# Sliding-window attention and SiLU feed-forward on one core: a replanned order, tile 0's activations in another buffer, fewer idle products

## The chip, the core and the metric

The kernel runs on one core of a Trainium2 chip. The core has a matrix engine (TensorE, PE in the profile, whose weight loads are listed apart as PEld), a vector engine (VectorE, DVE), an activation engine (ScalarE, ACT), a general engine (GpSimd, POOL) and a queue engine (SyncE, SP). Each runs its own list of instructions in order and waits on semaphores for the others. Transfers are issued by POOL, SP or ACT and moved by 16 DMA engines. PE writes its products to PSUM, eight banks of 128 x 512 fp32 values. The metric is device time in microseconds, the median of several runs.

## The reference

Two stages follow each other: causal attention with a window of 64 keys, for 8 batches of 8 heads, 576 positions and 64 values a head; then a feed-forward layer over all 4608 tokens.

```python
scores = scale * np.matmul(q, k.transpose(0, 1, 3, 2))
mask = (rel >= 0) & (rel < window)          # rel = query position - key position, window = 64
scores = np.where(mask, scores, -1000000000.0)
attn = np.exp(scores - max); attn = attn / (attn.sum(-1) + 1e-09)
x = (attn @ v).transpose(0, 2, 1, 3).reshape(4608, 512)
h = x @ w_in                                 # 512 x 2048
out = (h / (1 + np.exp(-h))) @ w_out         # 2048 x 512
```

## The kernel before

**Tiles.** The 4608 tokens are nine tiles of 512. A block is 64 query positions; a tile has 8 blocks. A quad is four of the eight heads. A visit is the attention of one quad for 4 or 8 blocks: `scores` on PE (a block against the 128 keys before its end), `exp` on ACT, a mask on DVE, `values` on PE, then on DVE the reciprocal of the sums, the product with it, and a transpose (`turn_out`, called "cross" in the plan) into the tile's input `xts`. In tile 0 the mask is a product of `block` with `ident` that is added to the scores on PE.

**Products.** Tile 0 uses plain products: `first_plain` makes 16 groups of 128 x 512 (a pair of columns of `w_in` for one half of the tokens, 8 products of 256 columns each, over four chunks of the contraction; chunks 0 and 1 come from quad 0, chunks 2 and 3 from quad 1), `silu_plain` makes the activations on ACT, and `second_plain` makes 64 products of 512 columns into four banks. Tiles 1 to 8 use a scheme with seven products instead of eight, with sums of weights (`wsum1`, `wsum2`), of tokens (`xsum`) and of activations (`gsum`) made on DVE, and a copy between banks on ACT ("fork"), a kept copy ("keep") and additions on DVE ("join") between the products. The stretch in which tile 0 is finished while the attention for tile 1 is made is called the bridge here.

**Order.** Every operation is recorded in a plan; `ORDER` is a written list of about 1590 words, each an operation's number, its engine and its banks. The instructions of an engine stand in the order of that list, so an engine's first waiting instruction holds all behind it. The loads of queries, keys, values and weights are all issued by POOL.

**Idle products.** PE begins with products of zeros (`warm`, 128 x 512), and more of them stand between the first scores; there are 36.

**Names.** `nat_87` and `nat_86` are the keys and the queries of batch 0 for quad 0, `nat_89` and `nat_88` those for quad 1; 90 to 93 are those of batch 1. `vv_98` are the values of batch 0. `w_in_sb_63` to `66` are four column parts of `w_in`, each loaded in two transfers (one for chunks 0 and 1, one for 2 and 3). `es_84` and `es_85` are the exponentials of quads 0 and 1. ACT holds one table of functions at a time; exp and SiLU need different ones, and a table load stands ahead of the first activation that needs another.

## Time and profile before

| | before |
|---|---|
| time, median of 3 runs | 277.2 us (276.77 to 277.22) |
| span of the profiled execution | 275.0 us |
| PE busy | 264.7 us (96%) |
| DVE busy | 214.0 us (78%) |
| ACT busy | 195.6 us (71%) |
| POOL busy | 129.7 us (47%) |
| table loads on ACT | 18, 1283 ns each |
| first product of tile 0, first product of tile 1 | 17.74 us, 52.23 us |

The profile is of one execution; what it gives as time is the span from the first to the last instruction, 2.2 us under the median of the runs. A row of the timeline has its start in us, its length, engine, line, operation, the tiles written and read, the count of merged instructions, and in brackets how long the engine sat idle before it and what ended that. A busy PE is not PE at its peak: a product counts as busy until its result is out, so products that follow each other with small waits still look busy.

### The profile page before, as it was taken

Reading aid. Unit: us, or ns where it says so; the run is one execution under the profiler, and the core shown is the slowest. Engines: PE = TensorE matmul, PEld = TensorE weight load, DVE = VectorE, ACT = ScalarE, POOL = GpSimd, SP = SyncE. Lnnn points to the kernel's source line nnn. Section 1 sums busy time; section 2 is a strip of 40 time slices with the busy share of each in tenths; the row PEclk is TensorE's granted clock in tenths of the full one; section 3 lists DMA queues with packets and bytes.
Section 4 is the critical chain, followed back from the end, with each engine's and each line's share of the span. In section 5 each row is a group of like instructions: output and inputs, shape, how many; then the busy total and the mean of one; then the engine's idle time right before and its main releaser. Section 6 shows DMA issues by size and latency. Waiting matters only on the chain.

```text
span 275.0 us, 10018 instructions
## 1 busy us (share of the span) xinstructions
PE 264.7 (96%) x4335; PEld 218.0 (79%) x4342; DVE 214.0 (78%) x426; ACT 195.6 (71%) x361; POOL 129.7 (47%) x194
## 2 busy tenths in 40 slices
PE   7978999999999999999999999999999999999993
PEld 2557844688888888888888888888888888888882
DVE  3757578999996898889799999988867967824741
ACT  1555993699749993987499958893888489537910
POOL 7944566988959758596387335940000000000000
PEclk9999999999999999999999999999999999999999
DMA  6999999999999959999979998990400040003004
GB/s 106 167 190 210 198 191 172 144 198 157 118 151 209 127 56 97 242 122 87 93 179 159 83 126 122 136 121 2 155 0 2 6 155 0 2 29 127 0 2 157
DMA packets 101631, 31.62 MB, mean 115 GB/s; under 512 B 92368, under 2 KB 95440, under 8 KB 101584
## 3 DMA queue, kind: packets, MB, share of 16 engines
q0 software_dynamic: 96128, 21.51, 86.1%
q1 hardware_dynamic: 5456, 9.44, 9.7%
q8 instruction: 35, 0.57, 0.9%
q14 instruction: 12, 0.10, 0.1%
HBM read 42.99 MB, written 9.44 MB: 191 GB/s over the span
## 4 chain that ended last, share of the span: by engine, by line
PE 88%; ACT 4%; DVE 4%; issue 1%; ACTq 0%
PE room L519 36%; PE room L507 35%; PE room L292 4%; PE room L323 4%; PE room L450 4%; PE room L895 4%; PE room L464 2%; ACT es L307 2%; DVE o L338 1%; ACT L307 1%; ACT g L461 1%; DVE es L314 1%; DVE xt L442 1%; PE room L285 1%; ACT L461 0%
## 5 line engine op out<-in xcount | busy, mean ns | idle before, releaser
L529 ACT ACTIVATE g<-room 128x512 bf16<-128x512 f32 x96 | 53.6, 605 | 4.5 <-PE room L507 4.1
L507 PEld LDWEIGHTS <-wsum 128*128 128x128 bf16 x512 | 49.9, 98 | 7.2 <-issue 1.0
L519 PEld LDWEIGHTS <-gsum 128*128 128x128 bf16 x512 | 49.1, 98 | 6.2 <-DVE gsum L496 0.2
L507 PE MATMUL room<-xsum,wsum 128*128 128x256 bf16 x384 | 53.3, 272 | 0.5 <-ACT es L307 0.3
L307 ACT ACTIVATE es<-room 128x512 bf16<-128x512 f32 (+1 forms) x88 | 39.1, 533 | 14.2 <-PE room L292 9.6
L519 PE MATMUL room<-wsum,gsum 128*128 128x256 bf16 x384 | 48.4, 273 | 0.0
L507 PEld LDWEIGHTS <-w_in_sb 128*128 128x128 bf16 x384 | 37.2, 98 | 4.7
L519 PEld LDWEIGHTS <-g 128*128 128x128 bf16 x384 | 36.7, 98 | 4.6
L526 DVE TENSOR_TENSOR room<-room,part 128x512 f32<-128x512 f32 (+1 forms) x41 | 27.8, 684 | 13.7 <-ACT part L523 3.5
L227 POOL DMA_DIRECT2D nat<-in_k_dram x48 | 30.0, 631 | 15.1 <-DVE kT L265 11.4
L507 PE MATMUL room<-xt,w_in_sb 128*128 128x256 bf16 x256 | 36.8, 273 | 0.0
L519 PE MATMUL room<-w_out_sb,g 128*128 128x256 bf16 x256 | 35.7, 273 | 0.0
L227 POOL DMA_DIRECT2D nat<-in_q_dram x48 | 29.9, 637 | 9.7 <-DVE qT L268 6.1
L523 ACT COPY ot<-room 128x512 f32<-128x512 f32 (+1 forms) x23 | 13.3, 582 | 28.6 <-PE room L519 21.5
L235 POOL DMA_DIRECT2D vv<-in_v_dram x32 | 29.6, 940 | 5.0 <-DMA nat<-in_k_dram 1.7
L523 ACT COPY room<-room 128x512 f32<-128x512 f32 x40 | 23.3, 592 | 12.1 <-PE room L507 10.8
L526 DVE TENSOR_TENSOR fin<-room,part 128x512 f32<-128x512 f32 x32 | 21.6, 683 | 9.0 <-PE room L507 6.1
L523 ACT COPY part<-room 128x512 f32<-128x512 f32 x40 | 23.6, 598 | 6.4 <-PE room L519 3.2
L241 POOL DMA_DIRECT2D vv<-in_v_dram x24 | 22.3, 934 | 12.0 <-PE room L323 11.5
L314 DVE TENSOR_TENSOR es<-es,strip 128x1024 bf16<-128x1024 bf16 (+1 forms) x36 | 21.9, 626 | 6.7 <-ACT es L307 6.4
L338 DVE TENSOR_TENSOR o<-room,recips 128x896 bf16<-128x896 f32 (+2 forms) x36 | 25.9, 726 | 0.8
L496 DVE TENSOR_TENSOR gsum<-g,gsum 128x512 bf16<-128x512 bf16 x64 | 25.1, 415 | 0.4
(75 smaller groups left out, 376.8 us busy)
## 6 DMA issues: line engine op xcount, KB each, us to landing
out_dram<-ot SPq DMA_DIRECT2D x16, 512.0 KB, 3.9
vv<-in_v_dram POOLq DMA_DIRECT2D x56, 128.0 KB, 5.0
nat<-in_k_dram POOLq DMA_DIRECT2D x48, 72.0 KB, 4.0
nat<-in_q_dram POOLq DMA_DIRECT2D x48, 72.0 KB, 3.7
w_in_sb<-in_moe_w_in_dram POOLq DMA_DIRECT2D x8, 256.0 KB, 9.2
w_out_sb<-in_moe_w_out_dram POOLq DMA_DIRECT2D x8, 256.0 KB, 9.0
nat<-in_k_dram POOLq DMA_DIRECT2D x4, 288.0 KB, 8.0
nat<-in_q_dram POOLq DMA_DIRECT2D x4, 288.0 KB, 8.2
```

What stands on the lines that cost most here:

```text
L227: queue[e].dma_start(out=nats[b % 2][a][kk][32 * h:32 * h + 32].rearrange("p (n x) -> p n x", n=NB), in_=(q, k)[kk][b, 4 * a + h].rearrang ...
L235: queue[e].dma_start(out=vv[b % 2][:, :, 2 * g + 1, 0:D], in_=v[b, :, 128 * g:128 * g + 128].rearrange("h p d -> p h d"))
L241: queue[e].dma_start(out=vv[b % 2][:, :, 2 * g, 0:D], in_=v[b, :, 128 * g - 64:128 * g + 64].rearrange("h p d -> p h d"))
L307: nc.scalar.activation(out=es_part(a, blocks)[:, h], in_=banks[bank.idx][:, 0:64 * n], func=ACTF.Exp, scale=scale)
L314: nc.vector.tensor_mul(t, t, strip[:, s:s + n].rearrange("k n i -> k (n i)").unsqueeze(1).to_broadcast([128, 2, 64 * n]))
L338: nc.vector.tensor_mul(out, at_values(bank, n)[:, :, :, 0:D], recips[:, w:w + 2 * n].rearrange("k (t n) -> k t n", t=bank.wide).unsqueeze( ...
L496: nc.vector.tensor_sub(out=dst[2 * i - 1], in0=g(1, 2 - i), in1=dst[i - 1])
L507: nc.tensor.matmul(banks[bank.idx][:, 256 * i:256 * i + 256], lhsT=lhs(z, i), rhs=rhs(z), start=(start and i == 0 and z == 0), stop=(z == ...
L519: nc.tensor.matmul(banks[bank.idx][:, 256 * m:256 * m + 256], lhsT=lhs(m, i), rhs=rhs(i), start=(start and i == 0 and m == 0), stop=(stop ...
L523: copies[e](out=dst, in_=src)
L526: nc.vector.tensor_add(out=dst, in0=bank, in1=part)
L529: nc.scalar.activation(out=g_tile(pair, 256 * t, 256 * t + 256), in_=src.rearrange("k (f t) -> k f t", f=2), func=ACTF.Silu)
```

## The change

- `run` takes a function `load`, which it calls ahead of the first ACT operation of another table: an activation of one column of `tiny`. The table load then stands ahead of that activation and no longer ahead of the operation itself.
- The first constants are filled on DVE (`const_fills`) and no longer on POOL; `ident` is made with one select instead of two.
- Tile 0's input lies in `xts[0]` by halves of the tokens (`by_half`), its activations lie in the space of `gsum` (`g_first`) and no longer in `gall`.
- All 16 groups of `first_plain` are split in two parts, one for quad 0's chunks and one for quad 1's, and a part waits only for the token half that it reads. Before, four groups of the first half were split.
- Copies of `vv` may go to ACT or DVE alike; the last tile's stores may be issued by ACT.
- The `ORDER` list is another one throughout, with 16 idle products, all at the start.

```diff
+            if engine == "A" and op["table"] not in (None, table):
+                table = op["table"]
+                load(table)
...
 ORDER = (
-    "1D 9G 2D 74P7 3D 11G 69P2 72P5 13G 67P0 15G 68P1 73P6 5G 70P3 71P4 19G 7D 78P3 81P6 82P7 86P3 6G 10D 77P2 89P6 90P7 75P0 17G 76P1 80P5 12D 83P0 79P4 "
...
+    "0D 9G 69P2 95P7 11G 92P4 72P7 86P7 1D 2D 18G 91P4 17G 67P4 4D 5G 7D 94P4 3D 15G 6G 13G 10D 97P7 83P2 68P0 75P1 73P0 99P2 70P3 78P0 12D 20G 19G 29G "
...
-        nc.gpsimd.memset(strip[:, 0], 1.0)
...
     def const_ident(_):
-        nc.gpsimd.memset(ident, 1.0)
-        nc.gpsimd.affine_select(out=ident, in_=ident, compare_op=ALU.is_ge, fill=0.0, base=0, channel_multiplier=1, pattern=[[-1, 128]])
-        nc.gpsimd.affine_select(out=ident, in_=ident, compare_op=ALU.is_ge, fill=0.0, base=0, channel_multiplier=-1, pattern=[[1, 128]])
+        nc.gpsimd.affine_select(out=ident, in_=ident, compare_op=ALU.not_equal, fill=1.0, base=0, channel_multiplier=1, pattern=[[-1, 128]])
+
+    def const_fills(_):
+        nc.vector.memset(strip[:, 0], 1.0)
+        nc.vector.memset(ident, 0.0)
+        nc.vector.memset(tiny, 0.0)
...
+    def by_half(t):
+        return t.rearrange("k c t -> k (c t)").rearrange("k (h c t) -> k h c t", h=2, c=4)
...
-                    rhs=xts[j % NXT][:, c, lo:hi], start=(i == 0 and c == 0), stop=(c == 3), skip_group_check=True)
+                    rhs=by_half(xts[0])[:, lo // 256, c], start=(i == 0 and c == 0), stop=(c == 3), skip_group_check=True)
+
+    g_first = gsum.rearrange("k u n f t -> k (u n f t)").rearrange("k (g f t) -> k g f t", g=8, f=2)
...
-            nc.scalar.activation(out=g_tile(pr, lo, hi), in_=src[:, i], func=ACTF.Silu)
+            nc.scalar.activation(out=g_first[:, pr, :, lo:hi], in_=src[:, i], func=ACTF.Silu)
...
-                if j == 0 and k_ == 0 and g0 < SPLIT:
-                    half = [x for nb in range(4) for x in xt_done[nb][:1]] + [win[ft // 2][0] for ft in fts]
...
+                half = [x for nb in range(lo // 64, hi // 64) for x in xt_done[nb][:1]] + [win[ft // 2][0] for ft in fts]
...
-            st = p.add({"SP": 0.45}, lambda e, i=i, r0=r0, r1=r1, lo=lo, hi=hi: store(e, j, 2 * i + r0, 2 * i + r1, lo, hi), deps, 0,
+            st = p.add({"SP": 0.45, "ACT": 0.4} if last else {"SP": 0.45}, lambda e, i=i, r0=r0, r1=r1, lo=lo, hi=hi: store(e, j, 2 * i + r0, 2 * i + r1, lo, hi), deps, 0,
...
-    p.run(ORDER)
+    p.run(ORDER, lambda table: nc.scalar.activation(out=tiny[:, 1:2], in_=tiny[:, 0:1], func={"exp": ACTF.Exp, "silu": ACTF.Silu}[table]))
```

The list's rows tell a reader nothing, so three places are shown as the engines' instructions stand, without their waits.

POOL's list at the start of the program, before: all keys and queries of batch 0, then the masks, then the values.

```order
L224 DMA nat_87<-in_k_dram 128x1152
L224 DMA nat_86<-in_q_dram 128x1152
L224 DMA nat_89<-in_k_dram 128x1152
L224 DMA nat_88<-in_q_dram 128x1152
L184 MEMSET strip 128x64
L185 ISA
L185 AFFINE_SELECT strip<-strip 128x64
L187 AFFINE_SELECT strip<-strip 128x64
L235 DMA vv_98<-in_v_dram 128x8x64
L191 MEMSET ident 128x128
```

The same place after the change:

```order
L230 DMA nat_87<-in_k_dram 128x1152
L230 DMA nat_86<-in_q_dram 128x1152
L241 DMA vv_98<-in_v_dram 128x8x64 x2
L188 ISA
L188 AFFINE_SELECT strip<-strip 128x64
L190 AFFINE_SELECT strip<-strip 128x64
L230 DMA nat_88<-in_q_dram 128x1152
L194 AFFINE_SELECT ident<-ident 128x128
L230 DMA nat_89<-in_k_dram 128x1152
L241 DMA vv_98<-in_v_dram 128x8x64 x2
L251 DMA w_in_sb_63<-in_moe_w_in_dram 128x2x512
```

Two transfers of values moved ahead of quad 1's queries and keys, and the masks behind those two.

DVE's list from the first transposes to the first result of the attention, before:

```order
L255 STREAM_TRANSPOSE kT_97<-nat_89 128x18x32
L258 STREAM_TRANSPOSE qT_95<-nat_88 128x9x64
L273 COPY vv_98<-vv_98 64x8x64
L205 MEMSET vv_99 128x72
L206 MEMSET vv_99 64x8x32
L275 COPY vv_98<-vv_98 64x8x64
L273 COPY vv_98<-vv_98 64x8x64
L275 COPY vv_98<-vv_98 64x8x64
L334 RECIPROCAL recips<-room 128x8
```

The same place after the change:

```order
L261 STREAM_TRANSPOSE kT_96<-nat_87 128x18x32
L264 STREAM_TRANSPOSE qT_94<-nat_86 128x9x64
L279 COPY vv_98<-vv_98 64x8x64 x2
L281 COPY vv_98<-vv_98 64x8x64 x2
L264 STREAM_TRANSPOSE qT_95<-nat_88 128x9x64
L261 STREAM_TRANSPOSE kT_97<-nat_89 128x18x32
L281 COPY vv_98<-vv_98 64x8x64
L340 RECIPROCAL recips<-room 128x8
```

The four copies of the first values now stand ahead of quad 1's transposes, and these stand between the first values and their reciprocal.

ACT's list at the end of tile 8, before:

```order
L529 ACTIVATE g<-fin_81 128x2x256
L523 COPY room<-room 128x512
L529 ACTIVATE g<-room 128x2x256 x2
L523 COPY part_80<-room 128x512
L523 COPY ot<-room 128x2x256
L523 COPY ot<-room 128x256
```

The same place after the change:

```order
L534 COPY part_80<-room 128x512
L544 DMA out_dram<-ot 128x2x256
L534 COPY ot<-room 128x256
L534 COPY ot<-room 128x2x256
L544 DMA out_dram<-ot 128x2x256
L534 COPY ot<-room 128x2x256
L534 COPY ot<-room 128x256
```

Two stores moved from SP's list into ACT's, and two output copies from DVE's into ACT's.

On PE, the list after the change has 16 idle products, then the scores of quad 0 for all eight blocks, its first values, quad 1's first scores, two parts of `first_plain`, the values of quad 0's second half, quad 1's other scores and values with three more parts among them, and then 25 parts in a row, the first of which also needs quad 1's half. Before, quad 0's scores, quad 1's scores and three of the four values stand with 11 idle products among them, ahead of the first part. In the bridge the list has four times 7 of the 64 second products and a scores step, then 8, two parts of `first_plain`, 2, two values, 8, two values and 17.

48 lines of the change are left out of this document (21 added, 27 removed), and 118 rows, old and new, of the table ORDER.

## Prediction

> **What bounds the kernel now.** I read the page's head, its slices and the chain first, then busy time by stage.
>
> ```profile
> span 275.0 us, 10018 instructions
> PE 264.7 (96%) x4335; PEld 218.0 (79%) x4342; DVE 214.0 (78%) x426; ACT 195.6 (71%) x361; POOL 129.7 (47%) x194
> DMA  6999999999999959999979998990400040003004
> PE 88%; ACT 4%; DVE 4%; issue 1%; ACTq 0%
> ```
>
> ```profile
> 0.00:17.70 17.70, 14.68 (x274) 7.27 (x275) 9.19 (x21) 8.93 (x21) 13.43 (x28) 1.00 1.19 146
> 34.20:52.20 18.00, 17.01 (x284) 8.12 (x288) 14.99 (x38) 11.56 (x26) 12.57 (x21) 1.00 1.43 163
> 195.00:222.00 27.00, 27.00 (x479) 23.64 (x477) 21.31 (x42) 20.65 (x38) 0.00 (x0) 1.00 0.16 60
> ```
>
> From left: stretch, length, busy time of PE, PEld, DVE, ACT, POOL with counts, granted clock, DMA, GB/s. In the middle PE is busy for the whole stretch and carries the chain: there only fewer products or smaller waits could help, and the change removes no real product. What can be won lies ahead of tile 0's products, in the bridge, and behind the last product. In the first two the DMA digit is 9, so transfers pace the start.
>
> ```profile
> 1.39 7.60 PE L895 MATMUL room<-fill 128*128 128x512 bf16 x24 [1.39 <-DVE fill L213]
> 5.58 1.25 DVE L255 STREAM_TRANSPOSE kT<-nat 128x576 f32<-128x576 f32 x1 [0.48 <-DMA nat<-in_k_dram]
> 7.06 1.21 DVE L258 STREAM_TRANSPOSE qT<-nat 128x576 f32<-128x576 f32 x1 [0.22 <-DMA nat<-in_q_dram]
> 9.36 0.42 PE L292 MATMUL room<-qT,kT 32*128 32x64 bf16 x32
> 11.86 0.29 DVE L273 COPY vv<-vv 64x512 bf16<-64x512 bf16 x1 [0.74 <-DMA vv<-in_v_dram]
> 15.50 0.70 POOL L245 DMA_DIRECT2D w_in_sb<-in_moe_w_in_dram  x1 [1.21 <-DMA w_in_sb<-in_moe_w_in_dram]
> 20.24 0.54 POOL L248 DMA_DIRECT2D w_out_sb<-in_moe_w_out_dram  x1 [0.77 <-DMA w_in_sb<-in_moe_w_in_dram]
> 17.21 0.60 PE L323 MATMUL room<-vv,es 128*32 128x65 bf16 x52 [1.58 <-issue]
> 22.42 7.91 PE room L450 x71
> 30.61 3.67 PE L450 MATMUL room<-xt,w_in_sb 128*128 128x256 bf16 x32
> 52.23 1.04 PE L507 MATMUL room<-xt,w_in_sb 128*128 128x256 bf16 x8
> ```
>
> Transfers land one after the other: quad 0's keys and queries by 5.58 and 7.06, then quad 1's two and the first two transfers of values, these by 11.86, later the `w_in` parts. POOL's issue at 15.50 was released by the first of these parts, that at 20.24, three issues on, by the fourth. The first scores stand behind the idle products, which run to 1.39 + 7.60 = 8.99. PE becomes dense at 22.42 (that row is the chain's). Of tile 0's 128 first products 71 + 32 = 103 follow there, so 25 were done.
>
> **The start.** The bytes ahead of the first `w_in` part are the same eight transfers, so it should land near 15.3 and the fourth near 20.2 again; the change fills the time ahead with better work. Quad 0: the masks are behind two value issues on POOL, and `block` behind the masks on DVE, with the clearing of the second value buffer behind that, all ahead of the first transpose. Those rows are:
>
> ```profile
> 4.29 0.24 POOL L187 TENSOR_SCALAR_AFFINE_SELECT strip<-strip 128x64 bf16<-128x64 bf16 x1
> 4.48 0.92 POOL L235 DMA_DIRECT2D vv<-in_v_dram  x1
> L224 POOL DMA_DIRECT2D nat<-in_k_dram x4 | 2.3, 583 | 1.5 <-POOLq L972 0.8 <-DMA w_in_sb<-in_moe_w_in_dram 0.7
> 4.57 0.35 DVE L197 TENSOR_SCALAR block<-strip 128x512 bf16<-128x512 bf16 x1 [2.52 <-POOL strip L187]
> L206 DVE MEMSET vv<- 64x256 uint32 x2 | 0.5, 272 | 0.0
> 9.83 2.32 ACT L307 ACTIVATE es<-room 128x256 bf16<-128x256 f32 x8 [7.61 <-PE room L292]
> 16.54 0.45 DVE L442 STREAM_TRANSPOSE xt<-o 128x256 f32<-128x256 f32 x1
> L338 DVE TENSOR_TENSOR o<-room,recips 128x896 bf16<-128x896 f32 (+2 forms) x36 | 25.9, 726 | 0.8
> ```
>
> Two value issues of 0.92 replace two quad issues of 0.58, so the masks end near 5.1 instead of 4.53, `block` (0.35 and a fill) near 5.6, and with the clearing (0.27 and a short one) the key transpose starts near 6.1 instead of 5.58; the query transpose ends near 8.6 instead of 8.27. Since fewer idle products stand ahead, scores start near 8.9 instead of 9.36. A quad's transfer takes 7.06 - 5.58 = 1.5; two quads and two values took 11.86 - 7.06 = 4.8, so a value transfer takes 0.9, and the first two land near 8.9. Quad 0's first values can run near 10.7, but both transposes of quad 1 stand ahead of their reciprocal on DVE: the same six transfers are complete near 11.86 in either order, the last transpose ends near 13.1, a value copy behind it near 13.7. Reciprocal 0.2, product 0.73, transpose 0.45: 15.1, in time for the first `w_in` part. Two parts (0.9 us), quad 0's other values, quad 1's scores and values, three parts more, and the 25 in a row start when the fourth `w_in` part is there and quad 1's transpose is done, both near 20.2.
>
> At 20.2 there remain 27 of 32 parts, 108 products; before, at 22.42, 103. A product takes 7.91 / 71 = 0.111 us. The lead is 22.42 - 20.2 - 5 x 0.111 = 1.7 us. Lower bound 0.5 (the cover of a full DVE and ACT list gone, each wait 0.3 later through five steps), upper 2.4.
>
> **The bridge.** Its work from 22.42 is 103 products, 64 second products, 4 scores and 4 values.
>
> ```profile
> 48.09 2.33 PE L464 MATMUL room<-w_out_sb,g 128*128 128x512 bf16 x10
> L464 PE MATMUL room<-w_out_sb,g 128*128 128x512 bf16 x59 | 14.6, 380 | 0.6 <-issue 0.5
> 30.98 1.28 ACT L307 ACT_TABLE_LOAD   x1
> 32.28 0.94 ACT L307 ACTIVATE es<-room 128x256 bf16<-128x256 f32 x3
> L307 ACT ACT_TABLE_LOAD x9 | 11.5, 1283 | 1.1 <-PEq L972 0.9
> L529 ACT ACT_TABLE_LOAD x7 | 9.0, 1283 | 0.4 <-PE room L507 0.3
> L307 ACT ACTIVATE es<-room 128x512 bf16<-128x512 f32 x56 | 29.5, 613 | 2.2 <-PE room L292 1.9
> L307 ACT ACTIVATE es<-room 128x256 bf16<-128x256 f32 x32 | 9.6, 394 | 12.0 <-PE room L292 7.6 <-DVE xt L442 4.3
> L273 ACT COPY vv<-vv 64x512 bf16<-64x512 bf16 x5 | 3.1, 618 | 0.1
> w_out_sb<-in_moe_w_out_dram POOLq DMA_DIRECT2D x1, 256.0 KB, 8.1
> ```
>
> A second product takes (2.33 - 0.38) / 9 = 0.217. A scores or values step is 0.45, the 0.42 of the row at 9.36 and 0.03 to change over. The work is 103 x 0.111 + 64 x 0.217 + 8 x 0.45 = 28.9; the stretch to 52.23 is 29.8, so 0.9 us are waits. After the change I find two waits left: all four scores use the same four banks, so each waits for four exponentials of 0.3 (2.32 / 8) behind a table switch, about 0.1 past the seven products that cover it; and three copies of 0.62 on ACT for the last values, which by that spacing land near 43.4, hold the last two values by 0.4. Together 0.5, so 0.4 is won. The bounds are 0 and 0.9. The last `w_out` part was issued at 36.43 (the row of the transfers of that issue: 8.1 us) and landed near 44.5; after, three transfers of one head, each a quarter of a quad's 1.5 us, stand ahead: 45.6. Eight products need it, PE reaches them near 47, so it is hidden by about a microsecond.
>
> **Table loads and small edits.** All 16 loads of the two rows idled for 1.5 us together, 0.9 of it at program start. A load ahead of a one-column activation can give back 0.4 us, on an ACT with 79 us idle: 0 on the path. The 17 added activations are not in the trace; the two shapes of L307 differ by 0.219 for 256 columns, so one column is 0.394 - 0.219 = 0.175, 3.0 us in all, off the path outside the bridge, where at most 0.2 each at two switches shows (bounds 0 and 0.4; 0, since seven products cover a switch). The trace has the exp 0.02 us behind the load's end at 32.26. [...] Tile 0's activations in another space and the copies moved to DVE (0.29 each) free `gall` early; no row shows a wait for it, so 0, hidden by PE.
>
> **The tail.**
>
> ```profile
> 267.78 4.11 SPq L533 DMA_DIRECT2D out_dram<-ot  x5
> 269.96 0.69 DVE L523 COPY ot<-room 128x512 f32<-128x512 f32 x1 [0.45 <-PE room L519]
> 270.40 0.37 ACT L523 COPY ot<-room 128x256 f32<-128x256 f32 x1 [2.65 <-PE room L519]
> ```
>
> SP ended its issues at 271.89, 1.1 us behind the last copy, since two stores came together. After, the wide copy follows a product that ends three half products before the last (two before) and takes 0.58 on ACT; its store is out 0.4 us sooner. Against it stand two issues of about 0.4 on ACT, queued ahead of that copy. I take -0.3, bounds -0.6 and +0.5.
>
> **Tiles 1 to 8.** No product goes; the list is new. In it four copies between banks have only 8 products (0.89 us) between the product they read and the one that waits; such a copy takes 0.59 and two hand-overs, so each may cost 0.1 us: +0.3, bounds -1.0 and +2.0. Loads are better covered than before, by 17 us of products at least.
>
> **Sum.** -1.7 - 0.4 - 0.3 + 0.3 = -2.1; against the profiled span 272.9, and 275.1 against the runs, whose median is 2.2 above that span.
>
> **Rivals.** (1) The clock. Before, 36 idle products keep PE running; after, 16 end near 7.3, and until 20 PE works less than half the time, with idle stretches up to 1.9 us.
>
> ```profile
> 6.02 2.47 PEld L895 LDWEIGHTS <-fill 128*128 128x128 bf16 x12 [0.24 <-issue]
> ```
>
> Of the 24 first idle products the last 12 loads come 2.47 / 12 = 0.206 us apart, the first 12 took 6.02 - 1.39 = 4.63, 0.39 each: the full rate came after 4.6 us of dense work. If it falls in the start, dense work from about 18 loses half of 4.6, 2.3 us: 277.4. The idle stretch of 1.58 us ahead of 17.21 did not lower it, which speaks against it. [...] (2) The other side: the new list's waits in tiles 1 to 8. If one in-order wait of 0.44 us a tile appears, as a fork or a join that its cover of 8 products does not hide with ACT busy, eight tiles cost 3.5 us: 278.3; it decides against the change from 0.3 us a tile. For it: the copies with short cover; against it: 27.00 of 27.00 busy before under a list with the same kinds of distances. (3) The change doesn't advance the bridge: transfers land 2 us later than I place them, second products wait for `w_out`, and tile 1 starts at 52: 277.1. (4) Waits of tiles 1 to 8 shrink as well: 273.8.
>
> **How the numbers follow.** Forecast 0.50, (1) 0.14, (2) 0.14, (3) 0.08, (4) 0.14. The forecast's own range is 274.0 to 276.4. With the gains of (4) below, and the clock and transfers above, 80% lie in 273.4 to 277.9. No change means within 0.2%, about what a measurement of this kernel can tell, 276.65 to 277.75: parts of (1) and (3), 0.14. Slower: (2) and a bad case of (1), 0.18. Faster: 0.68.
>
> **What would show it.** Tile 0's dense products from about 20.2 and tile 1's first product near 50 show the start and the bridge right; a granted clock under full between 7 and 25 us shows (1); more PE idle, or ACT and DVE pieces in the chain between 52 and 250, show (2); second products waiting on `w_out` show (3). The forecast is wrong if the dense run starts after 21.5, or the distance from tile 1's first product to the last product, 218 us before, grows by over 2 us.

## The result: slower, and the profile after

The changed kernel takes 279.86 us (median of 20 runs, 277.82 to 282.31), the kernel before 276.83 us (20 runs, 275.46 to 279.18) on the same chips: a ratio of 1.0104, with a 95% interval from 1.0076 to 1.0132. The forecast was 275.1 us, with a range up to 277.9. It was wrong on the side as well as in the size. The profiled execution took 281.5 us, its span is 279.5; it is the third longest of the 20, 1.6 us above their median, so what its trace shows as lost is more than the 3.03 us between the medians.

The head of the page of the changed kernel, its slices for PE, granted clock and transfers, and its chain:

```profile
span 279.5 us, 9986 instructions
PE 263.2 (94%) x4317; PEld 217.6 (78%) x4322; DVE 215.6 (77%) x435; ACT 193.7 (69%) x371; POOL 128.9 (46%) x191
...
PE   8569999999999989999995999999999999999993
...
PEclk9959999999999999999999899999999999999999
DMA  6999999999999999891399995049904003000314
...
PE 61%; ACT 11%; DVE 8%; DMA 8%; POOL 7%; issue 4%; POOLq 0%; ACTq 0%; DVEq 0%
```

PE is as busy as before in microseconds, so the time lies between its products. The granted clock shows two dips, in the start and at 153 us; DMA and POOL, which had no share of the chain before, now have 15% of it.

PE in the start, and its first product of tile 1 (the timeline of after):

```profile
16.15 1.89 PE L459 MATMUL room<-xt,w_in_sb 128*128 128x256 bf16 x8 [2.46 <-DMA w_in_sb<-in_moe_w_in_dram]
17.97 0.63 PE L329 MATMUL room<-vv,es 128*32 128x65 bf16 x32
...
22.32 11.09 PE L459 MATMUL room<-xt,w_in_sb 128*128 128x256 bf16 x100
...
51.29 0.60 PE L518 MATMUL room<-xt,w_in_sb 128*128 128x256 bf16 x4
```

Eight products took 1.89 us; at full clock eight take 1.04 (a row of e15_spread below). The dense run begins at 22.32, not at 20.2; tile 1 begins at 51.29, 0.94 us ahead of before instead of 2.1. The rest is lost behind it: from there to the end of the last product it was 218.1 us before and is 223.7 now. The stretch from 52 to 250 us, before and then after (busy time of PE, PEld, DVE, ACT, POOL, clock, DMA share, GB/s):

```profile
52.00:250.00 198.00, 197.31 (x3403) 171.52 (x3402) 167.41 (x323) 153.88 (x278) 95.20 (x134) 1.00 0.98 107
```

```profile
52.00:250.00 198.00, 193.67 (x3356) 167.48 (x3355) 167.65 (x328) 152.47 (x285) 93.44 (x132) 0.99 0.96 103
```

PE stands 4.3 us in place of 0.7 in it, nearly all at two places, and runs 3.5 us at half rate behind the second of them. In the timelines of PE and DVE:

```profile
98.57 0.78 DVE L271 STREAM_TRANSPOSE kT<-nat 128x576 f32<-128x576 f32 x1 [1.79 <-DMA nat<-in_k_dram]
```

```profile
100.05 0.61 PE L530 MATMUL room<-wsum,gsum 128*128 128x256 bf16 x4 [1.35 <-DVE gsum L507]
...
153.50 0.41 PE L329 MATMUL room<-vv,es 128*32 128x65 bf16 x16 [2.87 <-DMA vv<-in_v_dram]
```

```profile
153.00:156.50 3.50, 3.00 (x29) 2.15 (x29) 2.50 (x7) 1.56 (x2) 2.21 (x4) 0.51 1.81 141
```

At 100 us a key transpose stands in DVE's list ahead of two sums and waits for its transfer; the sums are what PE needs. At 153 us PE waits for a transfer of values. Why it came late stands in POOL's timeline, beside DVE's row of the transpose that it names:

```profile
135.88 0.61 POOL L233 DMA_DIRECT2D nat<-in_k_dram  x1 [11.67 <-DVE kT L271]
...
145.97 1.00 POOL L241 DMA_DIRECT2D vv<-in_v_dram  x1
```

```profile
134.81 0.77 DVE L271 STREAM_TRANSPOSE kT<-nat 128x576 f32<-128x576 f32 x1
```

A load of keys may not overwrite its buffer before the transpose has read it. That transpose is late in DVE's new list, and DVE had no pause ahead of it; POOL stood 11.67 us with the load, and all loads behind it stood too. The value load in question was issued at 145.97 and landed at 153.46: the held loads were issued one behind the other, and it took 7.5 us to land (the five value loads of 128 KB issued between 140 and 152 us: 7.0 in the median), where in e3_loads below, without the hold, the median around this place was 5.4.

### The profile page after: what moved, and what is told of

Its sections match the earlier page's. It is cut to its first block, busy times and chain, and to the rows that moved or that the text cites. A ratio compares the mean times of both kernels' runs of the same rounds, so it can differ in the third digit from the quotient of the medians.

```text
span 279.5 us, 9986 instructions
## 1 busy us (share of the span) xinstructions
PE 263.2 (94%) x4317; PEld 217.6 (78%) x4322; DVE 215.6 (77%) x435; ACT 193.7 (69%) x371; POOL 128.9 (46%) x191
## 4 chain that ended last, share of the span: by engine, by line
PE 61%; ACT 11%; DVE 8%; DMA 8%; POOL 7%; issue 4%; POOLq 0%; ACTq 0%; DVEq 0%
PE room L530 24%; PE room L518 23%; PE room L459 5%; ACT g L540 5%; PE room L475 4%; DMA w_in_sb<-in_moe_w_in_dram 3%; DMA vv<-in_v_dram 3%; PE room L298 3%; POOL nat L233 2%; DMA nat<-in_k_dram 2%; PE room L329 2%; POOL vv L241 2%; ACT es L313 2%; DVE es L320 2%; DVE o L344 2%
## 5 line engine op out<-in xcount | busy, mean ns | idle before, releaser
L518 PE MATMUL room<-xsum,wsum 128*128 128x256 bf16 x384 | 53.9, 273 | 0.0
L530 PE MATMUL room<-wsum,gsum 128*128 128x256 bf16 x384 | 50.6, 275 | 1.3 <-DVE gsum L507 1.3
L518 PE MATMUL room<-xt,w_in_sb 128*128 128x256 bf16 x256 | 37.4, 273 | 0.1
L241 POOL DMA_DIRECT2D vv<-in_v_dram x32 | 29.5, 937 | 6.3 <-PE room L329 3.1
L534 ACT COPY ot<-room 128x512 f32<-128x512 f32 (+1 forms) x18 | 10.0, 566 | 23.7 <-PE room L530 18.2
L344 DVE TENSOR_TENSOR o<-room,recips 128x896 bf16<-128x896 f32 (+2 forms) x36 | 25.1, 719 | 0.5
L504 DVE TENSOR_TENSOR gsum<-g 128x1024 bf16<-128x1024 bf16 x32 | 21.5, 682 | 5.0 <-ACT g L540 4.1
```

The lines of the kernel that those rows point to most:

```text
L241: queue[e].dma_start(out=vv[b % 2][:, :, 2 * g + 1, 0:D], in_=v[b, :, 128 * g:128 * g + 128].rearrange("h p d -> p h d"))
L344: nc.vector.tensor_mul(out, at_values(bank, n)[:, :, :, 0:D], recips[:, w:w + 2 * n].rearrange("k (t n) -> k t n", t=bank.wide).unsqueeze( ...
L504: nc.vector.tensor_sub(out=gsum[:, u, 0:4:2], in0=gall[:, lo:hi + 1, :, 256:512], in1=gall[:, lo].rearrange("k f (t n) -> k t f n", t=2))
L518: nc.tensor.matmul(banks[bank.idx][:, 256 * i:256 * i + 256], lhsT=lhs(z, i), rhs=rhs(z), start=(start and i == 0 and z == 0), stop=(z == ...
L530: nc.tensor.matmul(banks[bank.idx][:, 256 * m:256 * m + 256], lhsT=lhs(m, i), rhs=rhs(i), start=(start and i == 0 and m == 0), stop=(stop ...
L534: copies[e](out=dst, in_=src)
```

## The experiments

Each was built on the changed kernel or on the one before, and timed beside the kernel before. The first table puts the profiled executions side by side, for it separates the start from the rest: the first product of tile 1, and the distance from there to the end of the last product, in us, worked out from the traces.

| kernel | time, median (runs) | ratio to before, 95% | tile 1 starts | from there to the last product |
|---|---|---|---|---|
| before | 276.83 (20) | 1 | 52.23 | 218.1 |
| changed | 279.86 (20) | 1.0076 to 1.0132 | 51.29 | 223.7 |
| e1_warm | 282.49 (6) | 1.0137 to 1.0227 | 50.44 | 225.3 |
| e2_before16 | 278.01 (12) | 1.0006 to 1.0060 | 52.10 | 218.4 |
| e3_loads | 277.11 (12) | 0.9983 to 1.0028 | 51.01 | 219.4 |
| e4_both | 280.01 (6) | 1.0060 to 1.0145 | 50.39 | 226.2 |
| e5_loads_turn | 276.50 (12) | 0.9990 to 1.0049 | 51.38 | 219.6 |
| e6_all | 280.46 (6) | 1.0104 to 1.0194 | 50.43 | 223.6 |
| e7_no_tiny | 283.91 (8) | 1.0239 to 1.0325 | 52.41 | 222.7 |
| e8_clock_kept | 278.45 (12) | 1.0025 to 1.0082 | 53.33 | 219.1 |
| e9_shift60 | 278.68 (11) | 1.0039 to 1.0100 | 52.67 | 219.5 |
| e10_before16 | 276.37 (12) | 0.9947 to 1.0004 | 53.22 | 218.2 |
| e11_after_clock | 282.90 (6) | 1.0172 to 1.0251 | 52.14 | 225.2 |
| e12_clock82 | 279.44 (12) | 1.0041 to 1.0122 | 54.17 | 219.0 |
| e13_half82 | 277.61 (12) | 0.9999 to 1.0054 | 52.73 | 218.3 |
| e14_before_tiny | 277.21 (12) | 0.9962 to 1.0029 | 54.23 | 218.9 |
| e15_spread | 275.63 (12) | 0.9935 to 0.9980 | 49.49 | 219.6 |
| e16_spread_late | 275.77 (12) | 0.9938 to 0.9997 | 49.28 | 220.1 |
| e17_after_spread | 279.59 (6) | 1.0060 to 1.0158 | 49.64 | 222.5 |
| e18_loads_spread | 276.24 (12) | 0.9930 to 0.9997 | 49.73 | 220.2 |

### First set: the clock against the order of the loads

Two theories stood at the outset: the clock's fall in the start eats the lead (C), and the loads' order makes the two waits (L). e1_warm puts 20 idle products (fills, bank after the P) back:

```diff
-... 20G 19G 29G 157P3270 ... 162P2 27A 14D 26D 166P0675 ... 165D 196P0 193P3
+... 20G 19G 29G 71P3 74P3 76P3 157P3270 ... 162P2 27A 14D 26D 77P7 79P7 80P7 81P7 82P7 84P7 85P7 87P7 166P0675 ...
+    165D 88P6 89P6 90P6 93P6 96P6 98P6 100P6 101P6 102P6 196P0 193P3
```

> The changed kernel with 20 idle products put back into its three gaps in the start (3 ahead of quad 0's scores, 8 ahead of quad 1's, 9 ahead of the first w_in products), 36 in all as before. Theory C (the clock): the TensorE clock stays full from 12 to 20 us, tile 0's dense run starts 1 to 1.8 us earlier than in the changed kernel (near 21), and the time falls by about as much, 1.0 to 2.0 us. Rival W (the w_in transfers): the clock stays full as well, but the products that ran at the half rate wait for the next w_in part instead; the dense run still starts within 0.5 us of 22.3, and the time falls by less than 0.6 us.

e2_before16 takes from the old list the words of its last 20 idle products (eight of them are shown):

```diff
-... 75P0 17G 76P1 80P5 12D 83P0 79P4 84P1 18G 87P4 85P2 88P5 157P0123 ...
+... 75P0 17G 12D 18G 157P0123 ...
```

> The kernel before with the first 16 of its 36 idle products only. Theory C: the clock falls to half once in the start, for about 6.8 us, and the kernel becomes 1 to 2.5 us slower than before. Rival W: the clock falls, but the time stays within 0.6 us of before, since transfers pace the start. If the clock stays full, the old order's spacing of the work and not the number of idle products keeps it.

e3_loads moves three loads, which wait for late transposes, behind value loads that wait for nothing; e4_both is e1_warm and e3_loads in one:

```diff
-902D 1235G 870D ... 1232G ... 748G 908G 1239G 874S 1224G 913G 1228G 909G 914G 1070G
+902D 870D ... 748G 908G 874S 1224G 913G 1228G 909G 914G 1235G 1232G 1239G 1070G
```

> The changed kernel with three loads of keys and queries, which wait for late transposes, moved behind the four value loads that stood behind them in GpSimd's list. Theory L (in-order loads): the wait of 3.1 us for values at 153.5 goes, and with it the second fall of the clock; the time falls by 2 to 5 us in those runs that had both, by about 3 us at the median, while tile 1's first product stays near 51.3. Rival F (scattered waits on copies between banks): the wait goes, but others of the same sum take its place, and the distance from tile 1's first to the last product stays above 222 us.

> The changed kernel with both edits, the 20 idle products and the three moved loads. If C and L hold, the gains add up to 4 to 5 us, and the kernel ends at 275 to 276.5, faster than the kernel before by 0.3 to 2 us. If W and F hold, it stays above 278.5.

L held. With the loads moved, the value load is issued 14.8 us sooner, PE's wait at 153 us and the dip of the clock behind it are gone, and 2.75 of the 3.03 us come back: the ratio is 1.0006. POOL's timeline of e3_loads, then the stretch around the place in after and in e3_loads:

```profile
131.14 1.10 POOL L241 DMA_DIRECT2D vv<-in_v_dram  x1
```

```profile
135.00:165.00 30.00, 27.13 (x466) 23.07 (x465) 22.61 (x43) 20.24 (x39) 22.96 (x33) 0.94 1.35 129
```

```profile
135.00:165.00 30.00, 29.57 (x557) 25.22 (x555) 26.46 (x50) 23.50 (x45) 13.98 (x20) 1.00 1.00 118
```

C seemed to fall. With 20 idle products the dense run began at 20.87, 1.45 us sooner, and tile 1 at 50.44, as C has it, and yet both kernels with them took 2.6 and 2.9 us more than their twins without. The distance behind tile 1 grew by 1.6 us (e1_warm) and by 6.8 us (e4_both, whose profiled execution was the longest of its six). e2_before16 lost 0.9 us by its ratio, between what C and W had for it.

### Second set: what the idle products do to later tiles

e5_loads_turn is e3_loads with the transpose of 98 us moved behind two sums and a mask; e6_all is that with the 20 idle products of e1_warm; e7_no_tiny is the changed kernel without its one-column activations.

```diff
-667D 735D 664D 669D 680A 714D 684P
+667D 664D 669D 680A 714D 735D 684P
```

> The changed kernel with the three moved loads, and with one key transpose on VectorE, which at 98 us waits 1.8 us for its transfer ahead of two token sums, moved behind these sums and one mask. Theory L: PE's wait of 1.0 to 1.5 us for the sums at 99 to 100 us goes, no other of over 0.5 us takes its place, and the time falls by another 0.7 to 1.3 us below the kernel with the moved loads alone (277.1), to about 276. Rival P (transfers pace tiles 2 and 3): PE then waits for the scores that need the same transfer, and the time stays within 0.4 us of 277.1.

> The same as the last with the 20 idle products put back. Theory S (the idle products cost nothing by themselves, the start's lead of 0.6 to 0.9 us at tile 1 was only given back at the waits near 100 and 153 us): with these waits gone the lead is kept, and it is faster than the last kernel by 0.4 to 1 us. Rival N: the idle products make the later tiles slower whatever the waits, as in the two pairs run so far (2.6 and 2.9 us slower with them); it is 1.5 to 3 us slower than the last kernel, and its trace shows at which waits.

```diff
-    p.run(ORDER, lambda table: nc.scalar.activation(out=tiny[:, 1:2], in_=tiny[:, 0:1], func={"exp": ACTF.Exp, "silu": ACTF.Silu}[table]))
+    p.run(ORDER, lambda table: None)
```

> The changed kernel without the 17 one-column activations: each table load then stands directly ahead of the activation that needs it, as before the change. If they cost nothing on the path, as the forecast had it, the time is within 0.5 us of the changed kernel's 279.9. If a load ahead of time saves its 1.28 us at waits of PE, it becomes slower by up to 2 us; if the 0.2 us each on ScalarE's list count, faster by up to 1 us.

e5_loads_turn: PE's wait at 100 us is down to 0.34 us (excess over the usual spacing), but the time cannot be told from e3_loads (0.9990 to 1.0049 against 0.9983 to 1.0028). e6_all is 4.0 us slower than e5_loads_turn, though its tile 1 starts 0.95 us sooner, as rival N had it. Its trace shows where. PE stands in the middle of a scores step, with no releaser, that is, waiting for nothing in the program (the timeline of e6_all; behind it that of e5_loads_turn at the same work):

```profile
105.11 0.60 PE L298 MATMUL room<-qT,kT 32*128 32x64 bf16 x54
107.21 0.26 PE L298 MATMUL room<-qT,kT 32*128 32x64 bf16 x10 [1.50 <-issue]
...
153.03 0.67 PE L298 MATMUL room<-qT,kT 32*128 32x64 bf16 x62
155.59 0.20 PE L298 MATMUL room<-qT,kT 32*128 32x64 bf16 x2 [1.90 <-issue]
```

```profile
152.11 0.69 PE L298 MATMUL room<-qT,kT 32*128 32x64 bf16 x64
...
153.17 1.69 PE L530 MATMUL room<-wsum,gsum 128*128 128x256 bf16 x14
155.26 0.83 PE L530 MATMUL room<-wsum,gsum 128*128 128x256 bf16 x6 [0.40 <-issue]
```

The page of e6_all lists a DMA queue for instructions, 35 packets in 0.57 MB, 16 KB each; one of them lies between 152.5 and 155.5 us:

```profile
q8 instruction: 35, 0.57, 0.9%
```

```profile
q8 instruction: 1, 0.02, 1.9%
```

So I set each stall without a releaser beside the place of its instruction in PE's list (row 0 is the list's first) and the end of the last packet of that queue. "Stalled" is how much later its product starts behind the one before it than such products usually do, so it is somewhat more than the bracket, which counts from the end of that one:

| kernel | PE resumes at | stalled | row in PE's list | row mod 256 | after the packet's end |
|---|---|---|---|---|---|
| e6_all | 107.21 | 1.69 | 3518 | 190 | 1.50 |
| e6_all | 130.77 | 0.59 | 4286 | 190 | 1.42 |
| e6_all | 155.59 | 2.08 | 5054 | 190 | 1.70 |
| e6_all | 165.67 | 0.46 | 5566 | 190 | 1.33 |
| e6_all | 212.06 | 0.41 | 7102 | 190 | 1.43 |
| e5_loads_turn | 131.54 | 0.58 | 4286 | 190 | 1.42 |
| e5_loads_turn | 155.26 | 0.57 | 5054 | 190 | 1.41 |
| e5_loads_turn | 164.88 | 0.40 | 5566 | 190 | 1.47 |

All eight stand at a row with remainder 190: in these traces PE's instructions came in blocks of 256 (16 KB a packet, so 64 bytes each), 128 weight loads and 128 products, and PE went on 1.33 to 1.70 us after a block's packet had ended. The packet moved late: in e6_all PE passed the edge ahead of the stall of 155.59 at 150.66, the packet moved from 153.00 to 153.90. In 4.93 us PE used up a block of values, scores and few long products. In the traces of before and of the changed kernel a block's packet began to move between 1.87 us ahead of and 4.37 us behind PE's first product of the block before (34 packets in each). Where an edge falls, then, matters: 20 idle products are 40 instructions and push each edge 20 products back in the work, here into the scores. By the rows of this table the edges cost e6_all 5.2 us and e5_loads_turn 1.6, which makes 3.7 us of the 4.0; in the traces of before and of the changed kernel no edge behind 24 us stalls PE by over 0.3 us. Where the 2.08 us were lost the DMA engines were full: the DMA digit of e6_all is 9 in all 40 slices of 150.7 to 152.4 us and in 39 of the 40 of 152.5 to 155.5.

e7_no_tiny surprised more: 4.0 us slower than the changed kernel. Without the small activation a table load takes over the wait of the activation behind it. ACT's and PE's timelines of e7_no_tiny, and behind them ACT's of after, at the bridge's first scores:

```profile
35.42 1.28 ACT L313 ACT_TABLE_LOAD   x1 [1.32 <-PE room L298]
```

```profile
37.42 0.18 PE L298 MATMUL room<-qT,kT 32*128 32x64 bf16 x1 [0.48 <-ACT es L313]
```

```profile
34.06 1.28 ACT L958 ACT_TABLE_LOAD   x1
35.36 0.20 ACT L958 ACTIVATE tiny<-tiny 128x1 f32<-128x1 f32 x1
```

With it the load runs while ACT would wait anyway. By the groups of instructions the loads stood 9.1 us for others in e7_no_tiny (6.3 ahead of exponentials, 2.8 ahead of SiLUs), 1.5 before the change and 1.2 in after; tile 1 starts 1.1 us later without the small activations. The 4.0 us are a difference of medians: the profiled execution of e7_no_tiny is the shortest of its eight and as long as the changed kernel's (281.26 and 281.5), so the traces show where loads stand for others, but not where the whole 4.0 us go.

### Third set: the edges kept in place

e8_clock_kept is e5_loads_turn with the fills of e1_warm, each cut into four of a quarter of the columns, so that 128 products are added and every edge stays where it was. e11_after_clock is the same on the changed kernel, e9_shift60 cuts the 16 fills of e5_loads_turn into 76, and e10_before16 is e2_before16 with its 16 fills cut into 36.

```diff
-        nc.tensor.matmul(banks[op_bank.idx][:, 0:FILL], lhsT=fill[:, 0:128], rhs=fill[:, 0:FILL], start=True, stop=True)
+        for _ in range(times):
+            nc.tensor.matmul(banks[op_bank.idx][:, 0:cols], lhsT=fill[:, 0:128], rhs=fill[:, 0:cols], start=True, stop=True)
...
+# times, cols: e8, e11: 4, 128;  e9: 4 or 5, 104;  e10: 2 or 3, 224
```

> The kernel with the three moved loads and the moved transpose (276.5 us, clock at half for 6.8 us in the start), with idle work in the three gaps again, but as 36 x 4 products of 128 columns instead of 36 of 512: 128 products more than the 16 it had. Theory I (instruction blocks): TensorE's instructions come in blocks of 256, 128 weight loads and 128 products; a block's transfer starts when the block before it begins to run, and where 128 short products (scores, values) run out before it is there PE stands up to 2 us. 20 idle products more moved the blocks' edges into scores; 128 more leave every edge at the product where it was. Then the clock stays full, the lead of about 0.9 us at tile 1 is kept, the stalls between two scores products at 107, 155 and 166 us are gone, and it is 0.5 to 1.1 us faster than 276.5. Rival K (full clock or idle work in the start is itself what makes the later tiles slower): again 3 to 4 us slower than 276.5.

> The same base (276.5 us) with its 16 idle products of 512 columns cut into 76 of 104 columns, 7904 columns in all instead of 8192, so that the clock in the start and the start itself stay as they are and every block's edge falls 60 products earlier in the work. Theory I, worked out from the base's trace with 4.3 us from the start of a block to the next one at hand: stalls without a releaser near 75 us (3.0), 100 us (1.0), 183 us (1.4) and 206 us (1.3), in place of those near 131, 155 and 165 us (1.6 together); 4 to 7 us slower. Rival K: within 0.5 us of 276.5, since the clock and the idle time are the same.

> The kernel before without its last 20 idle products, the first 16 cut into 36 of 224 columns, so that every block's edge stays where it was. The clock falls in the start as in the changed kernel. Theory C (the half clock costs time in the start): 0.5 to 1.5 us slower than before. Rival W (transfers pace the start): within 0.4 us of before; then the 0.9 us that the run with 16 products of 512 columns lost are the moved edges'.

> The changed kernel with 36 x 4 idle products of 128 columns in the three gaps in place of its 16, nothing else moved. Theory I: the clock stays full in the start, edges stay, and it is 0.3 to 1.2 us faster than the changed kernel (279.9), as part of the lead is given back at the waits of 100 and 153 us. Rival K: as slow as with 20 idle products of 512 columns, 282.5.

Of the times, e10_before16's came as W had it, e11_after_clock's where rival K had it (282.90 against 282.5), though its trace shows another reason, and the other two missed. In e8_clock_kept the stalls of 1.69 and 2.08 us between scores products are indeed gone (the largest left at an edge behind tile 1's start is 0.54 us) and the distance behind tile 1 is that of e5_loads_turn less 0.5 us. But the start lost 1.95 us, for the idle products are instructions as well and brought an edge into quad 1's scores, where the DMA share was 1.54 (9.06 to 12.48 us) and 1.41 (12.48 to 15.89), with 180 and 192 GB/s (its timeline):

```profile
13.45 0.23 PE L298 MATMUL room<-qT,kT 32*128 32x64 bf16 x7 [0.45 <-DVE kT L261]
15.13 0.37 PE L298 MATMUL room<-qT,kT 32*128 32x64 bf16 x25 [1.45 <-issue]
15.98 3.74 PE L899 MATMUL room<-fill 128*128 128x128 bf16 x36 [0.48 <-ACT es L313]
```

The clock fell after that stop (1.00 up to 15.89, 0.50 from there to 19.30), so the fills of the last gap took 3.74 us and held the first w_in products up to 19.56. e11_after_clock shows two such stops (1.19 and 1.06 us) and, behind them, both waits of the changed kernel, with the clock at half for 6.83 us behind the second. e9_shift60 lost 2.2 us in place of 4 to 7: of the four stalls that I had worked out one came, 0.76 us at 77.68 in place of 3.0, since there the block was at hand 2.2 us after the edge and not after the 4.3 that I had taken for every block; one came where I had none, 0.65 at 135.26 (both at an edge, remainders 190 and 192). Why the other three did not come stays open. In the profiled executions its loss, 1.3 us, lies ahead of tile 1, and the distance behind it is that of e5_loads_turn: moving the edges by 60 products cost nothing there. e10_before16 is within 0.4 us of before, which is what W said. But its twelve executions differ in their clock: the two of mean 0.999 took 274.9 and 275.4, the two of 0.977 and 0.978 took 278.1 and 277.6. So in this list, too, executions with a long fall are some 2.7 us longer, and the median hides both kinds; with two of each, and the place of the fall known for the profiled one alone (11.07 to 21.31), this is a hint and no proof. e2_before16, with the edges moved, is 1.6 us slower than e10_before16; its trace has one stall at an edge that the other lacks, 0.54 us at 43.87, and the rest stays open.

### Fourth set: the clock alone

e12_clock82 and e13_half82 have 98 idle products each, in the first 40 ahead and 58 in the two gaps, in the second all ahead; base e5_loads_turn. e14_before_tiny is the kernel before with the change's hunk in `run`; the operation that fills `tiny` moves to the list's start, as the first activation reads it.

```diff
-        nc.tensor.matmul(banks[op_bank.idx][:, 0:FILL], lhsT=fill[:, 0:128], rhs=fill[:, 0:FILL], start=True, stop=True)
+        for _ in range(times):
+            nc.tensor.matmul(banks[op_bank.idx][:, 0:cols], lhsT=fill[:, 0:128], rhs=fill[:, 0:cols], start=True, stop=True)
...
+# e12: 40 of 204 columns ahead, 28 and 30 of 128 in the gaps;  e13: 98 of 88 columns ahead
```

> The kernel with the moved loads and the moved transpose (276.5 us), its idle work in 98 products: 40 ahead as now, 28 and 30 narrow ones in the two gaps of 1.9 and 2.5 us, sized so that they end before the scores and the first w_in part can run. Edges of instruction blocks fall 82 products earlier in the work, where by the base's trace about as little stands still as now (stalls of 1.7 us now; 1.5 by 4.3 us for a block). Theory C: the clock stays full in the start, tile 1 starts near 50.4 in place of 51.4, and it is 0.5 to 1.3 us faster than the next kernel, which has the same edges. Rival W: tile 1 starts within 0.4 us of the next kernel's, and the time is within 0.4 us of it.

> The same base and the same 98 idle products, all of them ahead of the first scores, 88 columns wide (8624 columns in all, in place of 8192): the clock falls in the start as in the changed kernel, the edges are those of the last kernel. Theory I: within 1 us of 276.5, with stalls without a releaser only near 75 us (1.0) and of under 0.5 us elsewhere. Rival K: as the last kernel but one that moved edges, 2 us slower.

> The kernel before with a one-column activation ahead of each change of table, which alone was taken out of the changed kernel and cost it 4.0 us. Theory T (the load no longer takes over the wait of the activation behind it; what that is worth depends on the list): in the old list the loads idled 0.6 us together outside the program's start, so within 0.5 us of before. Rival: 1 to 4 us faster, the part is worth the same in the old list.

The pair was spoilt as well: an edge now stood among tile 0's first products, and e12_clock82 stalled 2.1 us at it and lost its clock (0.50 from 23.07 to 26.48; its timeline), e13_half82 0.5. So e12_clock82 is 1.8 us slower than e13_half82, where C had it faster; e13_half82 itself lost 1.1 us against its base, just past the 1 us that theory I had for it, and the stall that was worked out near 75 us did not come.

```profile
19.66 0.72 PE L459 MATMUL room<-xt,w_in_sb 128*128 128x256 bf16 x5
22.47 1.14 PE L459 MATMUL room<-xt,w_in_sb 128*128 128x256 bf16 x7 [2.09 <-issue]
```

What the pair does show is that added instructions can be dear in the start: from one edge to the next block it took 6.8 us there in e12_clock82 (15.64 to 22.47) and 6.5 in e8_clock_kept (8.63 to 15.13), so 256 instructions would have to last that long to hide it. e14_before_tiny is not different from before (0.9962 to 1.0029): the small activations gain nothing in the old list. They are worth 4.0 us in a list that was laid out with them. Its profiled execution, the longest of its twelve, shows what the old list's start can do: PE stood 2.13 us ahead of 17.50, at the edge where the kernel before stood 1.58, and the clock fell under tile 0's first products (two stretches, before and after the fall):

```profile
14.62:18.03 3.41, 1.28 (x98) 0.96 (x97) 1.54 (x5) 2.83 (x6) 0.80 (x2) 1.00 1.22 202
18.03:21.45 3.42, 3.42 (x52) 2.08 (x46) 1.94 (x7) 0.00 (x0) 1.99 (x4) 0.50 1.24 212
```

There tile 1 started at 54.23, 2.0 us later than in the kernel before.

### Fifth set: the same 16 idle products, elsewhere

e15_spread and e16_spread_late move words only, on e5_loads_turn: 7, 4 and 5 products, and 4, 5 and 7, ahead of the first scores and in the two gaps. e17_after_spread does what e15_spread does on the changed kernel itself, e18_loads_spread on e3_loads.

```diff
-    ... 18G 91P4 17G 67P4 4D 5G 7D 94P4 3D 15G 6G 13G 10D 97P7 83P2 68P0 75P1 73P0 99P2 70P3 78P0 12D 20G 19G 29G 157P3270 ...
-    162P2 27A 14D 26D 166P0675 ... 165D 196P0 193P3
+    ... 18G 91P4 17G 67P4 4D 5G 7D 3D 15G 6G 13G 10D 12D 20G 19G 29G 157P3270 ...
+    162P2 27A 14D 26D 94P7 97P7 83P7 68P7 166P0675 ... 165D 75P6 73P6 99P6 70P6 78P6 196P0 193P3
```

> The kernel with the moved loads and the moved transpose (276.5 us); its 16 idle products, 512 columns each, stay 16, but 7 stand ahead of the first scores, 4 in the gap of 1.9 us ahead of quad 1's scores and 5 in the gap of 2.5 us ahead of the first w_in part. Instruction count and edges in the later tiles are those of the base. Theory C: the clock stays full in the start, tile 1 starts near 50.4 in place of 51.4, no new stall appears behind it, and it is 0.5 to 1.1 us faster than 276.5, the first kernel of this series below the kernel before. Rival W: the clock stays full, and the time stays within 0.4 us of 276.5. If the clock falls all the same, the time is that of the base within 0.4 us, and what the clock costs stays open.

> The same with 4, 5 and 7. With so few idle products ahead the clock may not be full at the first scores. If the clock is full from 12 to 20 us: as the last kernel within 0.4 us. If not: the 7 products of the last gap run at half rate, end near 17 instead of 16.1, and it is 0.5 to 1.5 us slower than the last.

> The changed kernel with nothing but its 16 idle products spread (7 ahead, 4 and 5 in the two gaps). Theory C: the clock stays full in the start, tile 1 starts near 49.5 to 50.4 in place of 51.3. Theory L: as the waits for the transpose's transfer at 100 us and for the values at 153 us are set by transfers and not by PE, most of that lead is given back there; the time falls by 0 to 0.9 us from 279.9. If it falls by 1.5 us or more, the lead passes these waits.

> The best kernel of the series (275.6 us, 0.9957 of before) without the moved transpose, so with the three moved loads and the spread idle products alone. If the transpose's place costs what the trace shows at 100 us (0.6 to 1.5 us of waiting for token sums), it is 0.5 to 1.2 us slower, near 276.5. If that wait only moved elsewhere, it is within 0.4 us of 275.6.

The forecast of C came true at last. e15_spread takes 275.63 us, ratio 0.9957 (0.9935 to 0.9980): 0.9 us less than e5_loads_turn, and less than both kernels of the case. Its timeline:

```profile
11.20 1.89 PE L898 MATMUL room<-fill 128*128 128x512 bf16 x4
...
14.68 1.24 PE L898 MATMUL room<-fill 128*128 128x512 bf16 x5 [0.49 <-ACT es L313]
15.75 1.04 PE L459 MATMUL room<-xt,w_in_sb 128*128 128x256 bf16 x8
...
20.58 3.67 PE L459 MATMUL room<-xt,w_in_sb 128*128 128x256 bf16 x32
...
49.49 0.60 PE L518 MATMUL room<-xt,w_in_sb 128*128 128x256 bf16 x4
```

Not all went as I had it: here the clock was at half up to about 13.6 us (four idle products in 1.89 us, against five in 1.24 later), and full from there on. That is enough in this trace: the rate was full when tile 0's first products began. The dense run starts at 20.58, 1.74 us ahead of after's, and tile 1 at 49.49, 1.8 us ahead; behind it the distance is that of e5_loads_turn, with stalls at edges of 0.8 us together. e16_spread_late does as well (0.9938 to 0.9997).

That the gain is the clock's rests on the profiled executions and not on the times. Six of e15_spread's twelve executions have a mean granted clock of 0.996 or more, six of 0.988 or less, and both sixes take 275.6 us in the mean. One way in which a fall can cost nothing stands in the trace of e18_loads_spread: there it lasted from 7.96 to 14.78, the first w_in products ran at full rate from 15.98, and tile 1 started at 49.73. Whether the falls of e15_spread lay as early is not on record.

e17_after_spread, with both waits left in, is 0.3 us below the changed kernel and inside its interval: as expected, but it does not show why, for in its profiled execution, the shortest of its six, the waits came 1.9 us sooner as well, so the lead was not given back there. How much of it survives these waits stays open. e18_loads_spread differs from e15_spread by 0.6 us in the median and by 0.1% in the ratio, which their intervals do not tell apart: the transpose's place is not shown to matter.

## Why the prediction was wrong, point by point

**The start, 1.7 us.** The work came where I had placed it, the rate did not. I took the idle stretch of 1.58 us ahead of 17.21 in the old kernel, which did not lower the clock, as evidence against rival (1). That reading looks at the longest pause; what differs in the traces is how busy PE is over a step of 3.41 us. (That pause of 1.58 us, by the way, was an edge as well: row 448, 1.39 us after a packet's end.) In the trace of after the granted clock changes at 13.11, 19.93, 153.05 and 156.47 us, distances of 6.83, 133.12 and 3.41, so multiples of 3.41; among the experiments the half clock lasts 6.83 in e18_loads_spread (7.96 to 14.78) and 10.24 in e10_before16 (11.07 to 21.31). Three stretches of after, laid to these steps, then the emptiest of before ahead of tile 0's dense run, then two of e15_spread:

```profile
9.70:13.11 3.41, 1.32 (x56) 0.74 (x44) 3.17 (x5) 1.43 (x5) 2.85 (x5) 1.00 1.74 174
13.11:16.52 3.41, 0.95 (x34) 0.70 (x35) 1.58 (x4) 2.72 (x8) 1.41 (x3) 0.50 1.21 184
16.52:19.93 3.41, 3.41 (x76) 2.07 (x73) 1.14 (x3) 0.00 (x0) 1.56 (x4) 0.50 1.24 205
```

```profile
16.21:19.62 3.41, 2.36 (x95) 1.88 (x96) 2.42 (x9) 1.33 (x2) 1.26 (x2) 1.00 1.23 199
```

```profile
13.59:17.00 3.41, 2.92 (x79) 1.84 (x77) 1.56 (x4) 2.49 (x7) 1.41 (x3) 1.00 1.24 204
17.00:20.41 3.41, 3.08 (x124) 2.31 (x112) 2.77 (x6) 2.29 (x5) 1.52 (x3) 1.00 1.24 206
```

With 1.32 us busy of 3.41 the clock went to half for the next two steps, with 2.36 it stayed, and the longest pause in the first was 1.87 us. The lead, counted as I had counted it, was 22.42 - 22.32 - 5 x 0.111 = -0.5 us; with the clock at full from tile 0's first products on (e15_spread) it was 22.42 - 20.58 - 5 x 0.111 = 1.3, near the 1.7. So the fall of rival (1), which I gave 0.14, happened in the profiled execution, and probably in all 20: their mean granted clocks are 0.988 or lower, which is what two steps at half make. If all that separates e5_loads_turn from e15_spread is the clock, it costs 0.9 us by the medians, by the profiled executions 1.8 at tile 1; not the 2.3 that I had worked out for it. Nor does the old list always keep its clock, though where in the run it falls is not on record: of 137 executions of the kernel before, timed beside the experiments, 17 have a mean clock of 0.991 or less and a median of 279.1 us, 73 have 0.999 or more and 276.4.

**The bridge, 0.4 us.** Better than said: from the dense run to tile 1 it was 29.81 us with 103 first products and is 28.97 with 108, a gain of 0.84 + 0.55 = 1.4 us, above my bound of 0.9. By my rates the work alone, 108 x 0.111 + 64 x 0.217 + 8 x 0.45 = 29.5, is longer than the whole stretch now is; so I had taken the rates too large, and with them the old waits too small. Rival (3) did not happen: no second product waited for `w_out`.

**Table loads, 0.** In the old list they are worth 0 (e14_before_tiny). The sum did not suffer. But the new list's bridge, which I costed with loads that hide behind seven products, rests on them, and without them the changed kernel is 4.0 us slower in the median; the one-column activation takes 0.20 us, where I had worked out 0.175.

**The tail, -0.3 us.** From the end of the last product to the end of the span it was 275.04 - 270.36 = 4.68 us, now 279.47 - 274.98 = 4.49 (last products of before and of after, timelines): -0.2.

```profile
269.76 0.60 PE L519 MATMUL room<-w_out_sb,gsum 128*128 128x256 bf16 x4
```

```profile
274.16 0.82 PE L530 MATMUL room<-w_out_sb,gsum 128*128 128x256 bf16 x6
```

**Tiles 1 to 8, +0.3 us with bounds -1.0 and +2.0.** This step failed, and it carried the sign: +5.55 us in the profiled execution. The sentence that was wrong is "Loads are better covered than before, by 17 us of products at least". I had measured each load from the product that frees its buffer, and not from the place in DVE's list of the transpose that reads it, nor through POOL's list, in which one waiting load holds all behind it, nor the time that the held loads then need to be moved. Moving three words takes 2.75 us of the 3.03 back. Rival (2) had the right kind, in-order waits, and the right side, at the wrong place: not a fork or a join in each tile, but above all one load, at 135 us. The transpose at 98 us cost PE 1.35 us in the trace, but moving it changed no time that the intervals can tell.

Both tests that I had set for the forecast, a dense run that starts after 21.5 and a distance that grows by over 2 us, struck. With the loads moved and the idle products spread, e15_spread reaches 275.63 us, close to the forecast of 275.1, but that is partly luck: in its profiled execution the start gives 1.3 us (1.7 in the sum), the bridge 1.5 (0.4), tiles 1 to 8 lose 1.4 (0.3), and the tail gives nothing (0.3). What the forecast lacked was the list's own order, followed to the end.

## What to carry to other kernels

Follow a buffer's reuse through every in-order list that it passes, reader's list, issuer's list, queue, not from the product that frees it: one load that waits behind a late transpose held all others behind it for 11.67 us. When work is taken out of a gap, ask how busy PE is over the few microseconds around it (here 1.32 of 3.41 us, where the clock fell, and 2.36, where it held) and not how long its longest pause is, and if idle products are to stay, put the same number into the gaps. And treat PE's instruction count as a parameter: 20 products more or less at the program's start move every block's edge through all later tiles, and a comparison of two kernels that differ in it compares two placements of edges.

## What the runs showed of the hardware that was not expected

- PE's instructions came in blocks of 256 rows, by packets of 16 KB on a queue of their own (q8 on the pages of before, after and e6_all: 35 packets, 0.57 MB, 0.9% of the 16 DMA engines' span). Behind 52 us the 20 traces have 32 stalls of over 0.3 us without a releaser; 29 of them stand at a row with remainder 190 or 192, 1.25 to 1.70 us after a packet's end, the longest 2.08 us (the other three are one place of the old list, 0.36). From one edge to the next block at hand it took 3.2 to 5.5 us at these stalls (2.2 in one case), and 5.8 to 8.2 at those in the first 23 us.
- The clock fell to half with no pause of PE over 1.87 us in the step ahead (after, 9.70 to 13.11): in the traces, ahead of the last product, it fell after steps of 3.41 us in which PE was busy for 0.41 us (e9_shift60) to 1.72 (e2_before16), and held after all others, the least busy of them with 1.56 (e7_no_tiny, 150.65 to 154.06). The traces give no sharper limit. It stayed at half for 3.41 us (after, at 153.05), 6.83 (after, at 13.11) or 10.24 (e10_before16, at 11.07).
- In e7_no_tiny a table load stood waiting for the scores that the activation behind it reads (1.32 us ahead of 35.42); with an activation of one column in front the load of the changed kernel ran at once (34.06).
- The profile's granted clock can read full where products ran slowly: on the pages of before and after its first digit is 9, though the traces' clock records begin at 5.97 and 6.28 us, and in e15_spread it is 1.00 from 9.56 to 12.97, where four idle products took 1.89 us (at 11.20), against five in 1.24 from 14.68 on.
